# Two mixtures of experts behind an attention: all low weight parts on VectorE, a new order at the begin of a mixture, and one branch less per expert

## The chip, the cores and the metric

The kernel runs on one core of a Trainium2 chip. The metric is the device time of one execution in microseconds (us), of several executions of the same program, smaller being better. The engines are named as the profile names them: PE (matrix products), PEld (its weight loads), DVE (VectorE), ACT (ScalarE), POOL (GpSimd), SP (the queue that issues the plain DMAs). A q behind a name (PEq, POOLq) is the engine's sequencer, which handles branches and semaphores.

## The reference, cut to what matters

An attention with a learned bias gives 1152 tokens of 512 numbers. They go through two mixtures of experts, one after the other, each with 8 experts, of which each token is sent to one:

```python
logits = xn @ en.T / tau              # second mixture: x @ w_gate
expert_idx = np.argmax(logits, axis=1)
...
for e in range(E):
    mask = expert_idx == e
    h = np.maximum(x[mask] @ w1[e], 0.0)             # 512 -> 1024
    out[mask] = gate_w[mask, None] * (h @ w2[e])     # 1024 -> 512
```

The second mixture takes the first one's output as x, has a gate matrix of its own, and drops tokens over a capacity of 288 per expert. All is float32. How many tokens an expert gets is known only at run time.

## The kernel before, in words

**Stages.** The attention fills about the first 250 us. Its last steps already load and split the first expert's weights (`early`, L918) and route 7 of the 9 token tiles. Then `moe` (L1210) routes the rest, runs the first mixture (`run(0, router)`), computes the second mixture's gate from the rows written (`gate2`, L1168) and runs the second mixture (`run(1, router)`). From L1213 on the order on every engine is the order of the program text.

**High and low parts.** Products are made at near float32 accuracy from a fast format: each weight piece (128 x 1024) is split by `hi` (L886, the rounded copy) and `lo` (L900, the raw piece minus the high part), and each product is the sum of three (`TERMS`, L575: high by high, high by low, low by high). An expert has eight pieces: 0 to 3 are w1, 4 to 7 are w2. The argument `eng` names the engine: A is ACT, V is DVE, G is POOL. `lo` frees its raw buffer and so issues, on SP, the DMA of the same piece of the next expert (`load`, L872). The tokens and the hidden values are split in the same way out of PSUM, always by ACT (high) and DVE (low): `halves` (L943) and `part` (L986).

**One tile.** `tile` (L961) computes up to 128 tokens of one expert: product 1 in two halves (`mm1`), the turn of the hidden values, product 2 (`mm2`, L991), scaling on ACT (L1020) and a scatter by an indirect DMA from POOL (L1027). Between its steps it calls `work(0)` to `work(5)`. In `run` (L1070), `work` splits the pieces of the *next* expert, of which piece 7 goes to POOL (high at step 0, low at step 4) and the others to ACT and DVE. At step 4 `turn` (L939) turns the tokens of the next tiles, and POOL gathers tokens ahead by indirect DMAs (`gather`, L928): the first tile of expert e+2 at step 0, the second tile of expert e+1 at step 4.

**Branches.** Each expert's first tile always runs. A second and further tiles stand in nested `tc.If` blocks (`more`, L1150, the If at L1161), which all engines evaluate; `announce` (L1145) gives PE a hint of the coming branch. Before the first tile, L1138 and L1139 put the gather of a *third* tile under an If of its own.

**Begin of a mixture.** `run` turns the router's result into lists and counts (`lists`, L788), gathers the first tokens, loads the counts into registers (L1078), lets PE run some products for nothing (`warm`) and calls `gates` (L799): an exponential on ACT, then on DVE a sum, a reciprocal and two spreads into `Bv` (`spread`, L716). Just before the second spread the first tile's tokens are turned. PE uses `Bv` in `gates2` (L824), called at step 1 of the first expert's tile, between its two halves of product 1. In the first mixture, the low parts of pieces 3, 6 and 7 of expert 0 go to POOL behind that, those of 4 and 5 to DVE.

**Between the mixtures.** In the last expert's tile of the first mixture, `held` (L877) lets only pieces 4 and 5 be loaded, since the raw buffers 0 to 3 take the first mixture's rows. Pieces 6 and 7 of the second mixture's first expert (number 8) are split at the end of `gate2` (L1195 to L1198) and in `run` (L1090), their low parts on POOL. Right behind them `gate2` calls `choose`, `place` and `spots`, a chain of small DVE instructions that gives the second mixture's lists.

Of the kernel before, what the change touches and what calls it, by code (L numbers as in the profile page):

```python
# [10 lines left out]
F16 = mybir.dt.float16  # L11
# [3 lines left out]
ALU = mybir.AluOpType  # L15
# [3 lines left out]
P = 128  # L19
B, H, S, D = 2, 8, 576, 64  # L20
BH = B * H
E8, FF = 8, 1024
# [548 lines left out]
NTT = NTOK // P  # L571
# [124 lines left out]
class Router:  # L696
# [99 lines left out]
        else:  # L796
            V.tensor_scalar(self.cnt, self.ps[:, 72:80], g.cap, None, ALU.min)

    def gates(self, turn, then):  # L799

        nc, V = self.nc, self.nc.vector
        if self.norms is not None:
            V.tensor_scalar(self.norms, self.norms, 1e-6, None, ALU.add)
            V.reciprocal(self.norms, self.norms)
            V.tensor_tensor(self.d, self.d, self.norms.unsqueeze(2).to_broadcast([P, NTT, E8]), ALU.mult)
        nc.scalar.activation(self.d, self.d, AF.Exp)
        then()
        gt = self.T("gt", [NTT])
        V.tensor_reduce(gt, self.d, AX.X, ALU.add)
        V.tensor_scalar(gt, gt, 1e-9, None, ALU.add)  # L810
        V.reciprocal(gt, gt)
        g2 = self.T("g2", [2, NTT], F16)
        V.tensor_copy(g2[:, 0], gt)
        V.tensor_tensor(gt, gt, g2[:, 0], ALU.subtract)
        V.tensor_scalar(g2[:, 1], gt, 4096.0, None, ALU.mult)
        self.Bg = []
        for j in range(2):
            if j == 1:
                turn()
            V.tensor_tensor(self.oht, self.oh, g2[:, j].unsqueeze(2).to_broadcast([P, NTT, E8]), ALU.mult)  # L820
            self.Bg.append(self.T("Bv", [NTT, E8 * NTT], F16, 2))
            self.spread(self.Bg[j], 0, NTT, self.oht, self.th)

# [15 lines left out]
class Experts:  # L839
# [32 lines left out]
    def load(self, ge, j):  # L872

        if ge >= 2 * E8:
            return
        m, e = divmod(ge, E8)
        w = self.a[("m_w1", "n_w1")[m] if j < 4 else ("m_w2", "n_w2")[m]][e]  # L877
        if self.held is not None and j not in (4, 5):
            return
        q = (ge * 8 + j) % NRAW  # L880
        r = self.raw[ge, j] = (self.rp if q < 6 else self.sp).tile([P, 1024], F32, tag=f"raw{q}", name="raw")
        kc = 1 if j < 4 else 2
        w = w.rearrange("(k p) f -> p k f", p=P)[:, (j % 4) * kc:(j % 4 + 1) * kc, :]
        self.nc.sync.dma_start(r.rearrange("p (k f) -> p k f", k=kc), w)
# [54 lines left out]
    def turn(self, key):  # L939
        if key in self.px:  # L940
            self.px[key] = self.halves(self.px[key], key[0])
# [128 lines left out]
    def run(self, m, router):  # L1070

        nc = self.nc
        A, V, G = nc.scalar, nc.vector, nc.gpsimd
        L = self.lists[m] = router
        L.lists()
        self.gather(m, 0, 0, ("b", 0))
        self.gather(m, 0, 1, ("f", 0))
        _, counts = nc.values_load_multi_w_load_instructions(L.cnt[0:1, :], min_val=0, max_val=NTOK,  # L1078
                                                             skip_runtime_bounds_check_because="numbers of tokens")
        self.warm(m * E8, WARM[m][2])  # L1080
        L.gates(lambda: self.turn(("b", 0)), lambda: m or self.hi(0, 7, A))
        if m == 0:
            self.lo(0, 3, G)
            self.lo(0, 4, V)
            self.lo(0, 5, V)
            self.lo(0, 6, G)
            self.lo(0, 7, G)
        self.held = None
        if m == 1:
            self.lo(E8, 7, G)  # L1090
        self.gather(m, 1, 0, ("b", 1))
        for e in range(E8):
            n = m * E8 + e + 1

            def work(at, e=e, n=n):
                if at == 0:
                    if n == E8:
                        self.held, self.yt = True, []
                    self.hi(n, 0, A)
                    self.hi(n, 1, A)  # L1100
                    self.lo(n, 0, V)
                    self.lo(n, 1, V)
                    if n == E8:
                        self.rows(0)
                        self.rows(1)
                    self.gather(m, e + 2, 0, ("b", e + 2))
                    if e < E8 - 1:
                        self.hi(n, 7, G)
                elif at == 1:
                    if e == 0:  # L1110
                        L.gates2()
                    self.hi(n, 2, A)
                elif at == 2:
                    self.lo(n, 2, V)
                    self.hi(n, 3, A)
                    self.lo(n, 3, V)
                    if n == E8:
                        self.rows(2)
                        self.rows(3)
                        self.rows(4)  # L1120
                    if e == 0:
                        L.gates3()
                elif at == 3:
                    self.hi(n, 4, A)
                elif at == 4:
                    self.hi(n, 5, A)
                    self.lo(n, 4, V)
                    self.turn(("f", e))
                    self.turn(("b", e + 1))
                    self.gather(m, e + 1, 1, ("f", e + 1))  # L1130
                    if e < E8 - 1:
                        self.lo(n, 7, G)
                    self.lo(n, 5, V)
                if at == 4 and e < E8 - 1:
                    self.hi(n, 6, A)
                    self.lo(n, 6, V)

            with self.tc.If(counts[e] > 2 * P):  # L1138
                self.gather(m, e, 2, ("x", 2))  # L1139
            self.announce(m, e, 1, counts[e])  # L1140
            self.tile(m, e, 0, ("b", e), work)
            self.px["x", 1] = self.px.pop(("f", e))
            self.more(m, e, 1, counts[e])
# [24 lines left out]
def gate2(tc, g, ex, router):  # L1168

    nc = tc.nc  # L1170
# [4 lines left out]
    n = len(todo)  # L1175
    x, lT = {}, {}
    for t in range(n + 3):
# [14 lines left out]
        elif u >= 0:  # L1192
            v = u - (u > OWN)
            nc.tensor.transpose(pb[:, v * 16:(v + 1) * 16], lT[u], g.ident[0:16, 0:16])  # L1194
    ex.hi(E8, 6, nc.scalar)  # L1195
    ex.hi(E8, 7, nc.scalar)
    ex.lo(E8, 6, nc.gpsimd)
    ex.release(E8 + 1, [6])  # L1198
    nc.vector.tensor_reduce(router.lg, pv.rearrange("p t a e -> p t e a"), AX.X, ALU.add)
    nc.vector.tensor_tensor(router.lg, router.lg, own, ALU.add)  # L1200
    ex.warm(E8, WARM[1][4])
# [71 lines left out]
```

## Time and profile before

| what | value |
|---|---|
| device time, median of 3 runs | 659.82 us (657.37 to 660.79) |
| the profiled execution's own time | 658.62 us |
| its span, first to last instruction | 656.7 us |
| mean granted clock of PE | 0.966 of full speed |
| busy PE, DVE, ACT, POOL | 551.3, 475.0, 400.8, 343.3 us |

Durations below come from the profiled execution. Its time exceeds its span by 1.9 us, which lie outside the first and last instruction. A timeline line gives start, duration, engine, line of the kernel, operation, tiles written and read, shape, and in brackets the idle time before it with what ended it; "x2" merges instructions that follow each other.

### The profile page before, as it was taken

What the parts mean: (1) busy time and instruction counts of PE and PEld (TensorE: products, weight loads), DVE (VectorE), ACT (ScalarE), POOL (GpSimd) and SP (SyncE); (2) the same over time, 40 slices, a digit from 0 to 9 for tenths busy, and PEclk for the clock granted to TensorE, in tenths of its full rate; (3) what the DMA queues carried; (4) which work ended last, traced back from release to release, by engine and by line L of the source; (5) the groups of instructions that cost most, each with busy time, mean ns of one, the idle gap of its engine ahead of it and who ended that gap; (6) DMA issues with size and microseconds to landing.
All of it is one profiled execution on the core that took longest, in us unless ns stands there. A gap on an engine that the chain in (4) does not pass through costs nothing. (4 is left out here: it accounts for less than half of the span.)

```text
span 656.7 us, 13255 instructions
## 1 busy us (share of the span) xinstructions
PE 551.3 (84%) x4970; PEld 463.6 (71%) x4970; DVE 475.0 (72%) x702; ACT 400.8 (61%) x668; POOL 343.3 (52%) x290
## 2 busy tenths in 40 slices
PE   2446688887898999679999999989979999999892
PEld 2445577887887887467788788767757887777672
DVE  5789999999998886868951371289679725929660
ACT  4566877887888855358742443378527626648451
POOL 3997899988987262634552141144145513525430
PEclk9977988999999999889999999999999999999797
DMA  7922545101100772298971270168737734847700
GB/s 228 308 74 51 142 133 165 38 30 37 25 18 18 164 267 80 81 324 302 326 284 44 59 252 30 35 211 316 276 102 241 277 126 147 302 150 233 267 8 8
DMA packets 46871, 101.46 MB, mean 154 GB/s; under 512 B 10740, under 2 KB 12660, under 8 KB 46496
## 3 DMA queue, kind: packets, MB, share of 16 engines
q1 hardware_dynamic: 40640, 92.12, 43.2%
q0 software_dynamic: 5232, 7.49, 3.3%
q8 instruction: 64, 1.05, 0.7%
q14 instruction: 55, 0.45, 0.2%
q10 hardware_dynamic: 880, 0.35, 0.2%
HBM read 94.06 MB, written 13.67 MB: 164 GB/s over the span
## 5 line engine op out<-in xcount | busy, mean ns | idle before, releaser
L906 DVE TENSOR_TENSOR wl<-raw,wh 128x1024 fp32r<-128x1024 f32 x106 | 155.1, 1499 | 22.4 <-ACT wh L893 17.4
L959 PE MATMUL py<-wh,hT 128*128 128x512 f32 x400 | 141.4, 404 | 0.3 <-DVE hT L989 0.2
L893 ACT CAST wh<-raw 128x1024 fp32r<-128x1024 f32 x111 | 114.8, 1050 | 12.5 <-ACTq L1161 4.4
L989 DVE TENSOR_TENSOR hT<-pt,hT 128x512 fp32r<-128x512 f32 x50 | 34.5, 691 | 92.7 <-ACT hT L988 92.6
L272 POOL TENSOR_TENSOR btmp<-abst,xp 128x256 f32<-128x256 f32 x78 | 81.0, 1038 | 16.4 <-ACT abst L271 15.2
L959 PEld LDWEIGHTS py<-wh,hT 128*128 128x128 f32 x400 | 75.0, 188 | 16.0 <-DVE hT L989 1.1
L259 PE MATMUL pm<-wmov,mask 128*128 128x64 f16 x1296 | 58.7, 204 | 28.4 <-DVE wmov L234 12.3
L959 PE MATMUL py<-wl,hT 128*128 128x512 f32 x200 | 78.2, 391 | 0.0
L259 PEld LDWEIGHTS <-mask 128*128 128x128 f16 x1296 | 52.9, 106 | 33.5 <-DVE mask L246 22.9
L321 PE MATMUL s<-K,Q 128*128 128x288 f32 x320 | 64.2, 326 | 13.8 <-DVE mx L329 10.3
L273 POOL TENSOR_TENSOR bias<-abst,btmp 128x256 f32<-128x256 f32 x78 | 72.0, 923 | 5.8
L246 DVE TENSOR_TENSOR mask<-toep,T 128x1024 f16<-128x1024 f16 x72 | 69.6, 984 | 0.8 <-PE pm L259 0.5
L339 ACT ACTIVATE P<-sb,mx 128x576 f32<-128x576 f32 x72 | 55.8, 776 | 23.0 <-DVE mx L329 19.3
L271 ACT ACTIVATE abst<-pm,swi 128x512 f32<-128x512 f32 x78 | 53.0, 685 | 21.9 <-PE pm L259 20.6
L959 PE MATMUL ph<-wh,xh 128*128 128x512 f32 x120 | 52.1, 434 | 15.6 <-PEq L1161 10.2
L353 PE MATMUL pt<-ident,P 128*128 128x128 f32 x324 | 53.5, 287 | 9.5 <-DVE ptl L364 6.0
L329 DVE CUSTOM_DVE_ANT_0 sb<-s,bias 128x576 f32<-128x576 f32 x72 | 53.7, 748 | 8.0 <-PE s L321 4.5
L364 DVE SCALAR_TENSOR_TENSOR ptl<-pt,pth 128x512 f16<-128x512 f32 x81 | 54.8, 680 | 5.2 <-ACT pth L359 5.0
L321 PEld LDWEIGHTS s<-K,Q 128*128 128x128 f32 x320 | 47.7, 198 | 15.1 <-issue 9.2
L906 POOL TENSOR_TENSOR wl<-raw,wh 128x1024 fp32r<-128x1024 f32 x22 | 52.7, 2398 | 6.2 <-ACT wh L893 5.5
L359 ACT ACTIVATE pth<-pt 128x512 f16<-128x512 f32 x81 | 47.6, 592 | 8.4 <-PE pt L353 7.1
L988 ACT CAST hT<-pt 128x512 fp32r<-128x512 f32 x50 | 29.4, 587 | 34.3 <-PE pt L983 30.4
(216 smaller groups left out, 1191.0 us busy)
## 6 DMA issues: line engine op xcount, KB each, us to landing
raw<-m_w_dram SPq DMA_DIRECT2D x64, 512.0 KB
raw<-n_w_dram SPq DMA_DIRECT2D x64, 512.0 KB
kraw<-a_k_dram SPq DMA_DIRECT2D x16, 288.0 KB
qraw<-a_q_dram SPq DMA_DIRECT2D x16, 256.0 KB
out_dram<-zero SPq DMA_DIRECT2D x9, 256.0 KB
y_tok<-zero SPq DMA_DIRECT2D x9, 256.0 KB
vraw<-a_v_dram SPq DMA_DIRECT2D x2, 1024.0 KB
x_tok<-x SPq DMA_DIRECT2D x8, 256.0 KB
```

Of the source, the lines that this page charges most:

```text
L246: nc.vector.tensor_tensor(m, w, T[:, i0:i0 + P].unsqueeze(1).to_broadcast([P, 8, P]), ALU.is_gt)
L259: nc.tensor.matmul(pm[:, :, :, gq * 4:gq * 4 + 4], m[:, gq], wmov[:, part], start=part == 0, stop=part == 1)
L272: nc.gpsimd.tensor_tensor(tmp, ab_[:, 0], xp, ALU.mult)
L273: nc.gpsimd.tensor_tensor(biases[it][:, :, cs], ab_[:, 1], tmp, ALU.add)
L321: nc.tensor.matmul(ps[:, half, :288], Q[:, part, h], K[:, b * H + h, half * 288:half * 288 + 288], start=i == 0, stop=i == last)
L329: nc.vector.tensor_tensor_reduce(sb.rearrange("p (t j) -> p t j", t=2), o.ps.pop(h)[:, :, :288], biases[o.it][:, h].rearrange("p (t j) -> ...
L339: nc.scalar.activation(o.Pt[hp][:, x * S:(x + 1) * S], sb, AF.Exp, bias=mx, scale=-1.0, accum_out=o.sums[:, h:h + 1])
L353: nc.tensor.transpose(pt[:, cc], src, ident)
L364: nc.vector.scalar_tensor_tensor(tl[:, ccs], o.pt.pop(h)[:, ccs], PSC, th[:, ccs], ALU.mult, ALU.subtract)
L893: eng.copy(hi, r)
L906: eng.tensor_tensor(lo, self.raw.pop((ge, j)), hi.bitcast(F32), ALU.subtract)
L959: self.nc.tensor.matmul(ps, x[a_][:, xs], w[b_][:, ws], start=first and i == 0, stop=last and i == 2)
```

## The change

All low parts in the two mixtures go to DVE. At the begin of the first mixture they are put between the parts of `gates`, which is cut into three. Pieces 6 and 7 of expert 8 are split in the last expert's tile of the first mixture, and their loads' successors are no longer held back there. The third tile's gather stands without an If.

```diff
--- before.py
+++ after.py
@@ -796,7 +796,7 @@
         else:
             V.tensor_scalar(self.cnt, self.ps[:, 72:80], g.cap, None, ALU.min)
 
-    def gates(self, turn, then):
+    def gates_exp(self):
 
         nc, V = self.nc, self.nc.vector
         if self.norms is not None:
@@ -804,20 +804,25 @@
             V.reciprocal(self.norms, self.norms)
             V.tensor_tensor(self.d, self.d, self.norms.unsqueeze(2).to_broadcast([P, NTT, E8]), ALU.mult)
         nc.scalar.activation(self.d, self.d, AF.Exp)
-        then()
+
+    def gates_sum(self):
+
+        nc, V = self.nc, self.nc.vector
         gt = self.T("gt", [NTT])
         V.tensor_reduce(gt, self.d, AX.X, ALU.add)
         V.tensor_scalar(gt, gt, 1e-9, None, ALU.add)
         V.reciprocal(gt, gt)
-        g2 = self.T("g2", [2, NTT], F16)
-        V.tensor_copy(g2[:, 0], gt)
-        V.tensor_tensor(gt, gt, g2[:, 0], ALU.subtract)
-        V.tensor_scalar(g2[:, 1], gt, 4096.0, None, ALU.mult)
+        self.g2 = self.T("g2", [2, NTT], F16)
+        V.tensor_copy(self.g2[:, 0], gt)
+        V.tensor_tensor(gt, gt, self.g2[:, 0], ALU.subtract)
+        V.tensor_scalar(self.g2[:, 1], gt, 4096.0, None, ALU.mult)
+
+    def gates_spread(self):
+
+        V = self.nc.vector
         self.Bg = []
         for j in range(2):
-            if j == 1:
-                turn()
-            V.tensor_tensor(self.oht, self.oh, g2[:, j].unsqueeze(2).to_broadcast([P, NTT, E8]), ALU.mult)
+            V.tensor_tensor(self.oht, self.oh, self.g2[:, j].unsqueeze(2).to_broadcast([P, NTT, E8]), ALU.mult)
             self.Bg.append(self.T("Bv", [NTT, E8 * NTT], F16, 2))
             self.spread(self.Bg[j], 0, NTT, self.oht, self.th)
 
@@ -875,7 +880,7 @@
             return
         m, e = divmod(ge, E8)
         w = self.a[("m_w1", "n_w1")[m] if j < 4 else ("m_w2", "n_w2")[m]][e]
-        if self.held is not None and j not in (4, 5):
+        if self.held is not None and j < 4:
             return
         q = (ge * 8 + j) % NRAW
         r = self.raw[ge, j] = (self.rp if q < 6 else self.sp).tile([P, 1024], F32, tag=f"raw{q}", name="raw")
@@ -1078,16 +1083,23 @@
         _, counts = nc.values_load_multi_w_load_instructions(L.cnt[0:1, :], min_val=0, max_val=NTOK,
                                                              skip_runtime_bounds_check_because="numbers of tokens")
         self.warm(m * E8, WARM[m][2])
-        L.gates(lambda: self.turn(("b", 0)), lambda: m or self.hi(0, 7, A))
+        self.held = None
         if m == 0:
-            self.lo(0, 3, G)
+            self.lo(0, 3, V)
+        L.gates_exp()
+        if m == 0:
+            self.hi(0, 7, A)
             self.lo(0, 4, V)
             self.lo(0, 5, V)
-            self.lo(0, 6, G)
-            self.lo(0, 7, G)
-        self.held = None
-        if m == 1:
-            self.lo(E8, 7, G)
+            L.gates_sum()
+            self.turn(("b", 0))
+            self.lo(0, 6, V)
+            self.lo(0, 7, V)
+            L.gates_spread()
+        else:
+            L.gates_sum()
+            L.gates_spread()
+            self.turn(("b", 0))
         self.gather(m, 1, 0, ("b", 1))
         for e in range(E8):
             n = m * E8 + e + 1
@@ -1104,8 +1116,7 @@
                         self.rows(0)
                         self.rows(1)
                     self.gather(m, e + 2, 0, ("b", e + 2))
-                    if e < E8 - 1:
-                        self.hi(n, 7, G)
+                    self.hi(n, 7, G)
                 elif at == 1:
                     if e == 0:
                         L.gates2()
@@ -1128,15 +1139,12 @@
                     self.turn(("f", e))
                     self.turn(("b", e + 1))
                     self.gather(m, e + 1, 1, ("f", e + 1))
-                    if e < E8 - 1:
-                        self.lo(n, 7, G)
                     self.lo(n, 5, V)
-                if at == 4 and e < E8 - 1:
                     self.hi(n, 6, A)
                     self.lo(n, 6, V)
-
-            with self.tc.If(counts[e] > 2 * P):
-                self.gather(m, e, 2, ("x", 2))
+                    self.lo(n, 7, V)
+
+            self.gather(m, e, 2, ("x", 2))
             self.announce(m, e, 1, counts[e])
             self.tile(m, e, 0, ("b", e), work)
             self.px["x", 1] = self.px.pop(("f", e))
@@ -1192,10 +1200,6 @@
         elif u >= 0:
             v = u - (u > OWN)
             nc.tensor.transpose(pb[:, v * 16:(v + 1) * 16], lT[u], g.ident[0:16, 0:16])
-    ex.hi(E8, 6, nc.scalar)
-    ex.hi(E8, 7, nc.scalar)
-    ex.lo(E8, 6, nc.gpsimd)
-    ex.release(E8 + 1, [6])
     nc.vector.tensor_reduce(router.lg, pv.rearrange("p t a e -> p t e a"), AX.X, ALU.add)
     nc.vector.tensor_tensor(router.lg, router.lg, own, ALU.add)
     ex.warm(E8, WARM[1][4])
```

## Rows read from the trace of the kernel before

**Rows 1.** Busy time by engine in two stretches (PE, PEld, DVE, ACT, POOL), clock, DMA.

```profile
273.70:276.70 3.00, 2.94 (x22) 2.24 (x23) 2.97 (x5) 0.83 (x2) 0.27 (x1) 0.50 0.04 10
...
305.80:319.10 13.30, 13.13 (x64) 10.53 (x64) 12.46 (x12) 10.26 (x15) 7.34 (x6) 1.00 0.90 309
```

**Rows 2.** What PE waited for, 250 to 480 us (total us, times, longest).

```profile
PE ph L959 <- PEq L1161: 5.3, 4, 3.3
PE ph L975 <- DVE xl L954: 5.2, 1, 5.2
...
PE pt L948 <- DVE hT L989: 0.8, 1, 0.8
...
PE ph L959 <- DVE xl L954: 0.5, 1, 0.5
```

**Rows 3.** What PE waited for, 480 to 660 us.

```profile
PE ph L959 <- PEq L1161: 5.0, 4, 3.0
...
PE pr L747 <- DVE oh L742: 2.5, 1, 2.5
```

**Rows 4.** Timeline of PE: begin of the first mixture, and where three experts begin.

```profile
273.76 2.08 PE L975 MATMUL ph<-wh,xl 128*128 128x512 f32 x4 [5.25 <-DVE xl L954]
275.63 1.30 PE L829 MATMUL pr<-Bv,A 128*128 128x72 f16 x18
...
290.51 0.66 PE L959 MATMUL ph<-wh,xh 128*128 128x512 f32 x1 [3.32 <-PEq L1161]
...
305.80 0.49 PE L959 MATMUL ph<-wh,xh 128*128 128x512 f32 x1 [0.66 <-PEq L1161]
...
319.75 0.48 PE L959 MATMUL ph<-wh,xh 128*128 128x512 f32 x1 [0.81 <-ACTq L1161]
```

**Rows 5.** Timeline of DVE at the begin of the first mixture.

```profile
261.60 0.17 DVE L803 TENSOR_SCALAR ss<-ss 128x9 f32<-128x9 f32 x1 [0.97 <-DVE cnt L795]
...
264.37 6.75 DVE L810 TENSOR_SCALAR gt<-gt 128x9 f32<-128x9 f32 x1
...
273.88 0.83 DVE L720 TENSOR_TENSOR Bv<-oht,th 128x648 f16<-128x648 f16 x1
```

**Rows 6.** Timeline of POOL: low parts, a gather, a high part.

```profile
264.06 7.01 POOL L906 TENSOR_TENSOR wl<-raw,wh 128x1024 fp32r<-128x1024 f32 x3
...
428.53 1.04 POOL L934 DMA_INDIRECT xgb<-x_tok,si  x1 [4.51 <-PE pt L983]
429.60 1.07 POOL L895 TENSOR_SCALAR wh<-raw 128x1024 fp32r<-128x1024 f32 x1
...
434.08 2.41 POOL L906 TENSOR_TENSOR wl<-raw,wh 128x1024 fp32r<-128x1024 f32 x1
...
479.49 2.36 POOL L906 TENSOR_TENSOR wl<-raw,wh 128x1024 fp32r<-128x1024 f32 x1 [5.51 <-ACT wh L893]
```

**Rows 7.** Timeline of DVE later on.

```profile
428.97 3.91 DVE L906 TENSOR_TENSOR wl<-raw,wh 128x1024 fp32r<-128x1024 f32 x2
...
433.41 4.18 DVE L906 TENSOR_TENSOR wl<-raw,wh 128x1024 fp32r<-128x1024 f32 x1
...
466.98 0.69 DVE L954 TENSOR_TENSOR xlx<-pt,xhx 128x512 fp32r<-128x512 f32 x1 [2.47 <-ACT xhx L953]
...
479.65 2.29 DVE L739 TENSOR_TENSOR d<-lg,mx 128x72 f32<-128x72 f32 x1
```

**Rows 8.** The low parts by line L906 on DVE: ns min/median/max, first to last start.

```profile
L906 DVE TENSOR_TENSOR wl<-raw,wh x106: 1208/1218/4179, 274.6 to 631.5; 128x1024 fp32r<-128x1024 f32 x106
```

**Rows 9.** The page's costliest groups: busy us, mean ns, idle before.

```profile
L893 ACT CAST wh<-raw 128x1024 fp32r<-128x1024 f32 x111 | 114.8, 1050 | 12.5 <-ACTq L1161 4.4
L989 DVE TENSOR_TENSOR hT<-pt,hT 128x512 fp32r<-128x512 f32 x50 | 34.5, 691 | 92.7 <-ACT hT L988 92.6
```

**Rows 10.** Timeline of ACT at the end of the first mixture.

```profile
464.83 0.69 ACT L1020 ACTIVATE xgf<-py,gs 128x512 f32<-128x512 f32 x1 [2.18 <-PE py L959]
```

**Rows 11.** Line L1138 on PE's sequencer, 299 to 308 us.

```profile
L1138 PEldq COMPARE_BRANCH  x1: 224/224/224, 305.3 to 305.3; - x1
```

## The prediction

> **What bounds the kernel now.** I read the stretches first: in an ordinary tile of the first mixture PE is busy 13.13 of 13.30 us, at full clock [rows 1]. So only time in which PE stands still, or runs at the low clock, can be won in the mixtures, and the next view is what PE waited for. Before 480 us that is 5.2 us for one low part of the first tokens, 5.3 us in four waits behind the branch at L1161, and 0.8 and 0.5 us for DVE [rows 2]; after 480 us it is 5.0 us behind that branch and 2.5 us for the router's chain [rows 3]. Next come the timelines around these waits.
>
> The 5.2 us stand at the begin of the first mixture: PE goes on at 273.76 after an idle 5.25 [rows 4]. DVE was held there by an addition on 9 numbers per partition that took 6.75 us, from 264.37 to 271.12 [rows 5], while POOL ran three low parts in a row from 264.06 to 271.07 [rows 6]. Both ended together: DVE could not start until POOL's run was over. The same shows at the router's chain: L739 took 2.29 us and ended at 481.94 [rows 7], beside POOL's low part of 479.49 to 481.85 [rows 6]. And in the tiles: a low part on DVE takes 1.22 us in the median but up to 4.18 [rows 8]; that longest one started at 433.41 [rows 7], when a low part of POOL was about to start at 434.08 [rows 6], and the waits of 0.8 and 0.5 us [rows 2] lie right behind it.
>
> **The change part by part. Begin of the first mixture.** DVE can start at 261.60 [rows 5]. Its new list is: low part 3, 1.22; three small instructions, 0.7 (estimate, four times the 0.17 of the first [rows 5]); low parts 4 and 5, 2.44; the sum and its followers with the tokens' low part and both spreads; then low parts 6 and 7, 2.44, between these. Freed at 271.12, DVE ended that middle work at 273.88 + 0.83 = 274.71 [rows 5], so it takes 3.6, with 0.4 for the reduction and the addition that come ahead of it 4.0. The sum is 1.22 + 0.7 + 2.44 + 4.0 + 2.44 = 10.8 us, and the last spread ends at 272.4 against 274.71.
>
> The tokens' low part comes out of this at about 268.5, which is when PE wants it (273.76 less 5.25). That wait goes. But PE's next stop is L829, which needs both spreads, and these now stand behind all five low parts: PE gets there near 269.6 and waits until about 272.4. L829 then ends near 272.8, where it ended at 276.7 before (the next product follows 1.1 us behind 275.63 [rows 4]). Of 5.25 us, 3.9 are won and the rest becomes a wait for `Bv`. Against that stands POOL, which in this stretch has four gathers and a high part of piece 7 to issue, each about 1.05 us [rows 6], and these too can hold DVE: two low parts took 3.91 us from 428.97 [rows 7], not 2.4, beside a gather and a high part [rows 6]. Three such holds take 3.1 back. So the bounds are 0.8 and 3.9; I take **2.4**, the middle, since POOL's gathers and DVE's low parts fall in the same 8 us but not all on each other. The clock lies inside this: it was at 0.50 (1.2 GHz) in the 3 us behind the wait [rows 1], and may be so behind the new one. SP gets the loads behind pieces 3 to 7 earlier by these same few us, and the gather of expert 1 no longer stands behind three low parts in POOL's queue; nobody waits for either, so this counts as nothing.
>
> **The rule on that lock.** The rows show DVE waiting out three POOL instructions. The Trainium skill (SBUF — State Buffer, on the shared port pair) says that a VectorE instruction with two SBUF inputs or in a two-port mode and a GpSimd instruction exclude each other, each for the whole of one instruction, whoever starts first. Taken to the letter, DVE would get in after the first of the three, 2.4 us, and a sum by the page would then have about 1.4 us for the begin (2.4 for the wait less the holds of about one short instruction). The trace has 6.75, so here a run of POOL instructions counts as one hold, and my sum goes by that.
>
> **The branch at L1138.** Its compare takes 0.224 us on PE's sequencer at 305.3 [rows 11], inside the 0.66 us that PE stands between two experts [rows 4]. With its neighbours I count 0.25 for each of 14 experts (the first of each mixture waits for its tokens anyway): **3.5**. Lower bound nothing, if another part of the way through L1161 ends last; upper 4.2, at 0.30. In exchange POOL runs the gather for every expert, 1.04 each [rows 6], with all rows out of bounds where there is no third tile. POOL queues behind it the gather of expert e+2 and the high part of piece 7; the gather has a whole tile of 14 us until it is turned, so I cost this at nothing. If that cover went, 1 us per expert would show.
>
> **The router's chain of the second mixture.** L739 was held from 479.65 until POOL ended at 481.85 and ran about 0.1 us beyond that, so 2.2 us of its 2.29 are hold; PE waits for this chain [rows 3], and I count **2.1**. The low part and two ACT casts that stood here go into the tile before. There a cast of 1.05 [rows 9] fits into ACT's idle 2.18 [rows 10], and two low parts, 2.4, fit just into DVE's idle 2.47 before the first tokens of `gate2` [rows 7]. Cost nothing, at most 0.5 if they come later. The two loads that go out earlier stand on SP behind the reads of the rows.
>
> **Piece 7 of the other experts** moves to DVE: 1.22 more per tile. In a tile DVE then has eight low parts, 9.8, and four reads of PSUM at 0.69 [rows 9], 2.8: 12.5 us beside a tile of 13.95 (319.75 less 305.80 [rows 4]). What it loses in work it wins in holds, since a hold by POOL's low part costs 2.4. So nothing, and the waits of 0.8 and 0.5 us [rows 2] go: **1.3**.
>
> **The sum.** 2.4 + 3.5 + 2.1 + 1.3 = 9.3. The profiled execution took 658.62 us, so 649.3; the median of the runs stands 1.2 above that execution, and I take 650.0.
>
> **Rivals.** *The waits behind L1161 change their number.* Two of the branches that skip further tiles cost far more than the others: 3.32 us at 290.51 [rows 4] and one of 3.0 us [rows 3], against 0.66. The tile behind the first took 15.29 us (290.51 to 305.80) where the next took 13.95, so one costs 2.7 + 1.3 = 4.0. All PE code behind the removed branch moves by a few instructions per expert, so these two can go, or others come: one less gives 646, two less 642, one more 654. For it: two of about a dozen show it with the same code, so something as small as place or moment decides. Against: nothing in the change aims at it. The Trainium skill (Runtime: NRT & Kernel Launch, instruction fetch mechanics) has a rule for it: a taken branch whose target is outside the window that is loaded stalls for a fetch. By that rule, a branch whose target lies near costs no fetch, and a sum by the page would have nothing for L1138 and 653 or so; the trace has 0.224 for it.
>
> *DVE becomes the bound of the tiles.* This is the one that ends slower. DVE needs 12.5 us of the 13.7 that a tile then takes. POOL now issues two gathers and a high part of piece 7 in a row in each tile, 3.2 us, and a run of POOL's holds DVE as a whole, as at the begin. It decides from 1.2 us of holds per tile on. If all 3.2 fell on DVE, each of the ten single tiles that prepare a next expert would take 2.0 longer: 650 + 20 = 670. Against: before, DVE carried the same holds and one of 2.4 us besides, and PE hardly waited for it [rows 2].
>
> *The branch was not the last in its gap, or the begin's wait only moves.* Then 3.5 or 2.4 us are missing: 653 or so, with both 656.
>
> *The change does nothing that PE sees,* because all of these gaps are set by something else: 660.
>
> **How the numbers follow.** The forecast (647 to 653) has 0.50; fewer waits at L1161 (640 to 646) 0.17; one more of them (653 to 658) 0.13; branch or begin empty (653 to 657) 0.12; DVE the bound (663 and more) 0.05; nothing 0.03. A measurement can tell 0.5%, 3.3 us, from no change, so faster means below 656.5 and slower above 663.1. Faster: 0.50 + 0.17, most of 0.13 and 0.12, 0.86 in all; same 0.09; slower 0.05. The range that leaves out 0.2 goes from 642, two waits less, to 656, both terms empty or one wait more with a weak begin.
>
> **What would show it.** In the new profile: L810 near 0.2 us; PE's 5.25 gone and a wait of 2 to 3 us at L829 for `Bv` in its place; L739 at a few tenths and PE's 2.5 us for it shorter; gaps of about 0.4 us between experts; low parts on DVE with a longest near 2.3 instead of 4.18. The prediction is wrong if PE waits for `hT` or `xl` in most single tiles, if the gaps stay at 0.66, or if the waits behind L1161 of 3 us are other than two.

## The result, and the profile after

The changed kernel takes 644.36 us (median of 4 runs, 643.15 to 646.07) against 658.6 (657.37 to 660.79) before: a ratio of 0.977, 95% interval [0.974, 0.980], so 14.2 us less. The prediction said 650.0, within 642 to 656. One of all executions reported below, in run 12, had a granted clock of 0.83 and took 676.38 us; it is left out. The profiled execution took 643.15 us, against 658.62. Its page begins so, and further down has the queue of the indirect DMAs:

```profile
span 641.4 us, 13184 instructions
...
PE 546.4 (85%) x4970; PEld 461.5 (72%) x4970; DVE 466.1 (73%) x721; ACT 399.8 (62%) x667; POOL 319.4 (50%) x285
...
q0 software_dynamic: 6272, 7.49, 3.6%
```

DVE has 19 low parts more, some 23 us at 1.22 each, and is still busy 8.9 us *less* (475.0 before): so about 32 us of its busy time before was waiting for POOL. The statistics of its low parts (ns, least, median and greatest, where [rows 8] stands for before) say the same:

```profile
L911 DVE TENSOR_TENSOR wl<-raw,wh x125: 1209/1218/2762, 261.7 to 617.2; 128x1024 fp32r<-128x1024 f32 x125
```

What PE waited for from 250 to 480 us, to be held against [rows 2]:

```profile
PE ph L964 <- PEq L1169: 4.6, 7, 1.7
PE pr L834 <- DVE Bv L720: 2.3, 2, 1.7
PE pt L953 <- DMA yt<-y_tok: 2.1, 1, 2.1
...
PE pr L747 <- DVE oh L742: 1.6, 1, 1.6
PE ph L964 <- issue: 0.8, 1, 0.8
```

and from 480 us to the end, against [rows 3]:

```profile
PE ph L964 <- PEq L1169: 3.2, 7, 0.6
```

No wait for `hT` or a token's low part is left. The two waits of 3 us behind the branch of further tiles (now L1169) are gone: 1.7 is the longest of seven before 480 us, 0.6 after it. In place of the first there are two stops, 1.74 and 0.83 us. New are the waits for `Bv`, which was foreseen, and for rows read back (`yt`), which was not. PE's timeline at the same places as [rows 4]:

```profile
268.40 1.08 PE L980 MATMUL ph<-wh,xl 128*128 128x512 f32 x4
271.14 0.45 PE L834 MATMUL pr<-Bv,A 128*128 128x72 f16 x9 [1.66 <-DVE Bv L720]
272.28 0.45 PE L834 MATMUL pr<-Bv,A 128*128 128x72 f16 x9 [0.68 <-DVE Bv L720]
272.56 0.48 PE L964 MATMUL ph<-wh,xh 128*128 128x512 f32 x1
...
284.61 0.49 PE L964 MATMUL ph<-wh,xh 128*128 128x512 f32 x1 [1.74 <-PEq L1169]
...
288.43 0.50 PE L964 MATMUL ph<-wh,xh 128*128 128x512 f32 x1 [0.83 <-issue]
...
299.13 0.50 PE L964 MATMUL ph<-wh,xh 128*128 128x512 f32 x1 [0.38 <-PEq L1169]
...
456.19 1.09 PE L953 MATMUL pt<-ident,yt 128*128 128x128 f32 x4 [2.14 <-DMA yt<-y_tok]
```

and DVE's at the begin and in the router's chain, as [rows 5, 7]:

```profile
263.43 2.35 DVE L911 TENSOR_TENSOR wl<-raw,wh 128x1024 fp32r<-128x1024 f32 x2
...
265.95 0.17 DVE L813 TENSOR_SCALAR gt<-gt 128x9 f32<-128x9 f32 x1
...
271.39 0.83 DVE L720 TENSOR_TENSOR Bv<-oht,th 128x648 f16<-128x648 f16 x1
...
471.75 0.23 DVE L1204 TENSOR_TENSOR lg<-lg,own 128x72 f32<-128x72 f32 x1 [1.17 <-DMA own<-l_tok]
472.28 0.23 DVE L739 TENSOR_TENSOR d<-lg,mx 128x72 f32<-128x72 f32 x1
```

**Where 15.3 us of span went.** I took the start of every tile's first ACT activation as a mark and compared the intervals between marks. Up to expert 2 the changed kernel gains 6.67 us: 4.18 by the first product behind `Bv` (272.56 against 276.74) and 2.49 around the first skipped branch and the gap behind it. Ten later intervals that hold one plain gap between experts are shorter by 3.32 in all, 0.33 each. Two more, the first tiles of the two experts with four tiles, are shorter by 0.74 together; they hold no such gap. The interval with the low parts of 3.91 and 4.18 us [rows 7] loses 2.09 (15.58 to 13.49), and the one with the second wait of 3 us 5.54 (18.98 to 13.44). Against that, `gate2`'s interval, from the last tile of the first mixture to the first of the second, is 1.68 longer (40.21 to 41.89), and the tail from the last mark to the end 1.35: 6.67 + 3.32 + 0.74 + 2.09 + 5.54 - 1.68 - 1.35 = 15.33, the 15.3 but for rounding.

### The profile page after: what moved, and what is told of

The parts are those of the page before. It is cut to its first block, busy times and chain, and to the rows that moved or that the text cites. A ratio compares the mean times of both kernels' runs of the same rounds, so it can differ in the third digit from the quotient of the medians.

```text
span 641.4 us, 13184 instructions
## 1 busy us (share of the span) xinstructions
PE 546.4 (85%) x4970; PEld 461.5 (72%) x4970; DVE 466.1 (73%) x721; ACT 399.8 (62%) x667; POOL 319.4 (50%) x285
## 3 DMA queue, kind: packets, MB, share of 16 engines
q0 software_dynamic: 6272, 7.49, 3.6%
## 5 line engine op out<-in xcount | busy, mean ns | idle before, releaser
L964 PE MATMUL ph<-wh,xh 128*128 128x512 f32 x120 | 50.1, 418 | 8.6 <-PEq L1169 7.7
L1033 POOL DMA_INDIRECT y_tok<-y,si x13 | 18.0, 1382 | 67.6 <-ACT y L1025 41.1
```

The costliest lines, as they stand in the source:

```text
L964: self.nc.tensor.matmul(ps, x[a_][:, xs], w[b_][:, ws], start=first and i == 0, stop=last and i == 2)
```

## The experiments

In the edits, `third` stands for `self.gather(m, e, 2, ("x", 2))`. Ratios are to executions of the kernel before that ran beside them; a version with one time and no ratio was executed once.

**1. The changed kernel with the branch back.**

```diff
-            third
+            with self.tc.If(counts[e] > 2 * P):
+                third
```

> The new kernel with the third tile's gather under its If again, all else as changed. Account of the two traces: each of 13 gaps between experts is 0.34 longer, 4.4 us; POOL's last drain goes back from 6.5 to about 5.5 us, since it grew with the number of indirect DMAs (13 empty gathers more), so 1.1 less at the end; and the rows for the second gate come about 1 us earlier. On the second wait of 3 us behind the branch over further tiles, which the change lost (5.2 us with its low clock), two theories: by place (PE's code is where it was before again) it returns and the time is about 651; by moment (the order on DVE and POOL decides) it stays away and the time is about 646. Rival of the whole: the branch cost PE nothing, and the time stays at 644.

652.6 us (651.22 to 655.08), ratio to before 0.990 [0.987, 0.993]. PE's timeline has the gaps of 0.66 again, and the second long wait. A wait for `hT` is back too, though every low part is still on DVE:

```profile
427.51 0.66 PE L953 MATMUL pt<-ident,xgb 128*128 128x128 f32 x4 [0.84 <-DVE hT L994]
...
609.13 0.79 PE L964 MATMUL ph<-wh,xh 128*128 128x512 f32 x1 [2.72 <-PEq L1170]
...
626.30 0.49 PE L964 MATMUL ph<-wh,xh 128*128 128x512 f32 x1 [0.66 <-PEq L1170]
```

The interval with the second long wait is 18.64 us (13.44 in the changed kernel), so the theory by place holds; the one with the wait for `hT` is 14.80 (13.49). The span from the last scatter's start to the end falls to 10.6 us, from 12.0.

**2. The kernel before without the branch, and nothing else.**

```diff
-            with self.tc.If(counts[e] > 2 * P):
-                third
+            third
```

> The kernel before with the gather's If taken away and nothing else. 13 gaps of 0.34 less, 4.4 us, and the drain 1.1 longer: about 655. By place, the second wait of 3 us behind the branch over further tiles goes too, and the time is about 650. If the branch was not the last in its gap: 658 to 660.

652.65 us (650.27 to 655.69), ratio 0.990 [0.987, 0.993]: between the two theories. In PE's timeline the second long wait is gone at the same expert, though run 1 has it at 609.13 and this run is there at 610.09, while the first stays:

```profile
290.65 0.49 PE L959 MATMUL ph<-wh,xh 128*128 128x512 f32 x1 [3.01 <-PEq L1160]
...
304.70 0.49 PE L959 MATMUL ph<-wh,xh 128*128 128x512 f32 x1 [0.38 <-PEq L1160]
...
610.09 0.49 PE L959 MATMUL ph<-wh,xh 128*128 128x512 f32 x1 [0.38 <-PEq L1160]
```

So the second wait goes with the branch, whatever the moment: it is there in all three profiles with the branch (before, 1 and 4), and in none of the eleven without it. The interval with POOL's low part of [rows 6] falls to 13.48 by this edit alone. What is missing to the lower theory lies in three intervals in which PE waits for `hT` or the next tile's tokens (0.75 to 1.1 longer than before each, with the one behind the first of them 0.8 longer), in `gate2` (41.51) and in a tail of 12.0. By the spans, the branch alone gains 6.2 us and all the rest of the change (before against run 1) 6.1, both together 15.3.

**3. The changed kernel with the old begin** (low parts 3, 6, 7 of expert 0 on POOL).

```diff
-            self.lo(0, 3, V)
...
-            self.lo(0, 6, V)
-            self.lo(0, 7, V)
...
+            L.gates_spread(lambda: self.turn(("b", 0)))
+            self.lo(0, 3, G)
...
+            self.lo(0, 6, G)
+            self.lo(0, 7, G)
```

> The new kernel with the begin of the first mixture as it was (low parts 3, 6 and 7 of expert 0 on POOL behind the gates, the tokens' turn ahead of the second spread). My account: DVE's addition takes 6.7 us again beside POOL's three low parts, PE waits 5.2 for the tokens' low part and none for the spreads, the first product behind the gates' products starts 4.2 later (276.7 instead of 272.6), and the time is about 648. Rival: the begin's gain is given back at the next branch, where the first wait of 3 us shrank only because of it; then up to 6 us, 650.

653.79 us, more than either theory said. The addition L813 takes 7.63 us and PE waits 5.23. The rest is at the first skipped branch, which waits 3.05, with a second stop in the tile behind it:

```profile
297.52 0.72 PE L966 MATMUL ph<-wh,xh 128*128 128x512 f32 x1 [1.93 <-issue]
```

**4. The kernel before, with only one low part on POOL at the begin.**

```diff
-            self.lo(0, 6, G)
-            self.lo(0, 7, G)
+            self.lo(0, 6, V)
+            self.lo(0, 7, V)
```

> The kernel before with low parts 6 and 7 of expert 0 on DVE behind the gates and only low part 3 on POOL. If DVE is held by each instruction of POOL for itself (page on SBUF), it should have got in after the first of three, so that the 6.75 had another cause and stays near 6.7. If a run of POOL counts as one hold, the hold shrinks to that one low part: the addition takes about 2.3 and PE's wait of 5.25 falls to about 0.8.

655.39 us. DVE's addition and POOL's low part, from the two timelines:

```profile
263.72 2.77 DVE L810 TENSOR_SCALAR gt<-gt 128x9 f32<-128x9 f32 x1
```

```profile
264.08 2.36 POOL L906 TENSOR_TENSOR wl<-raw,wh 128x1024 fp32r<-128x1024 f32 x1
```

Both end at 266.4 to 266.5. With one POOL instruction the hold is 2.77 us, with three in a row 6.75 [rows 5, 6]: a run of them holds as a whole. PE's wait for the token's low part falls from 5.25 to 0.61. But a wait of 2.82 for `hT` comes instead, since DVE now runs six low parts ahead of it.

**5. The changed kernel with the loads of pieces 6 and 7 held back in gate2.**

```diff
-        if self.held is not None and j < 4:
+        if self.held is not None and j not in (4, 5):
...
+    ex.release(E8 + 1, [6, 7])
     nc.vector.tensor_reduce(router.lg, pv...
```

> The changed kernel, but the loads of pieces 6 and 7 of the expert after next are held back until the second router's products are through, as in the kernel before (the casts and low parts stay where the change has them). The changed kernel's stage of gate2 is 1.7 us longer than before (41.9 against 40.2 us), with PE waiting 2.1 us for rows read back from y_tok and DVE 1.2 us for own logits. Theory of the earlier loads: they share the DMA engines with the scatter and the read-back; held back, both waits go and the stage falls to about 40, the run to about 642.5. Rival, the longer POOL queue (an extra gather ahead of expert 6's scatter): the waits stay, the stage stays at 41 to 42, the run at 644.

644.46 us; the stage takes 40.46. The wait for rows stays, and it is now followed by full clock in the table of stretches (the last three numbers are the granted clock, the DMA share and GB/s), where the changed kernel's fell. First the wait in PE's timeline, then the stretch:

```profile
458.76 0.63 PE L953 MATMUL pt<-ident,yt 128*128 128x128 f32 x4 [2.17 <-DMA yt<-y_tok]
```

```profile
458.00:461.00 3.00, 1.75 (x13) 1.34 (x13) 1.84 (x2) 1.07 (x3) 0.34 (x1) 1.00 1.02 357
```

The changed kernel, one stretch around its wait for the rows:

```profile
455.00:458.00 3.00, 1.81 (x8) 1.49 (x9) 1.25 (x2) 0.59 (x1) 0.79 (x1) 0.67 0.88 294
```

The own logits are waited for 0.82 instead of 1.17. So the earlier loads are not what delays the rows.

**6. The changed kernel with the spreads ahead of low parts 6 and 7.**

```diff
+            L.gates_spread()
             self.lo(0, 6, V)
             self.lo(0, 7, V)
-            L.gates_spread()
```

> The changed kernel, but at the begin of the first mixture the two spreads of the gates stand ahead of low parts 6 and 7 on DVE. In the changed kernel PE waits 1.7 + 0.7 us for the spreads, since two low parts of 1.2 us each stand ahead. Theory: this wait is the rest of the begin's cost; with the spreads first it falls to nearly nothing and the low parts are still there in time for the last products of the first tile, so 2 to 2.4 us less, about 642. Rival: the low parts 6 and 7 (or hT, which DVE reads behind them) are then late in the first tile, as with the one-low run, where the wait for hT took 2.8 us: same time, 644.

644.16 us (643.44 to 646.76), ratio to before 0.976 [0.973, 0.979]: no gain. PE's timeline, from the slowest of its executions (646.76), shows where it went:

```profile
271.62 0.45 PE L834 MATMUL pr<-Bv,A 128*128 128x72 f16 x9 [0.29 <-DVE Bv L720]
...
276.77 0.74 PE L964 MATMUL py<-wh,hT 128*128 128x512 f32 x2 [0.93 <-DVE hT L994]
...
285.64 0.49 PE L964 MATMUL ph<-wh,xh 128*128 128x512 f32 x1 [2.19 <-PEq L1169]
...
290.56 0.51 PE L964 MATMUL ph<-wh,xh 128*128 128x512 f32 x1 [1.90 <-issue]
```

The wait for `Bv` falls by 2.0, `hT` is 0.9 late as the rival said, and the two stops at the first skipped branch are 0.45 and 1.07 longer than in the changed kernel, whose PE program is the same.

**7. The third tile's gather moved into the second tile's branch.**

```diff
-            third
...
-                if at == 0 and t > 1:
+                if at == 0:
```

> The changed kernel without the branch around the third tile's gather, and without the gather being issued for every expert: it is issued in the second tile's work, inside the branch that tile has anyway. So PE still has no branch there, but POOL no longer issues a gather with all rows out of bounds where there is no second tile. Theory of the gathers' price: the drain at the end goes from 6.5 back to about 5.6 us and the last INC_SWDGE_SEM from 1.74 to 1.5 (1.0 to 1.2 us of the tail's 1.35), and expert 6's scatter, and so the rows of gate2, come about 1 us earlier: 642 in all, 641 at best. Rival: the third tile's gather now comes a tile later and the tiles behind it wait for it (three experts), and PE's code moves, so that one of the stops of 3 us behind L1169 comes back: 645 or more.

644.63 us (642.19 to 647.33), ratio to before 0.978 [0.975, 0.982]; the profiled execution has 642.19. The page's queue row and PE's timeline:

```profile
q0 software_dynamic: 5312, 7.49, 3.4%
```

```profile
455.44 0.66 PE L953 MATMUL pt<-ident,yt 128*128 128x128 f32 x4 [0.82 <-ACTq L1168]
```

The rows come in time, `gate2` takes 40.73 (41.89), and the tail is 10.9 (12.0). Two intervals in which PE turns a third tile's rows are longer by 0.30 and 0.57, one single tile by 0.28, and DVE waits 1.53 for the own logits (1.17). So both theories hold, and little is left. The queue carries 80 packets for each gather, also for one with all rows out of bounds: the changed kernel has 1040 packets and thirteen gathers more than the kernel before, and 1.35 us more of tail. All profiles agree on that tail: 10.6 us at 5232 packets (three of them), 10.9 at 5312 (three), 11.9 to 12.0 from 6112 to 6272 (eight).

**8. A ninth low part per tile on DVE.**

```diff
-        eng.tensor_tensor(lo, self.raw.pop((ge, j)), hi.bitcast(F32), ALU.subtract)
+        for _ in range(2 if j == 7 and ge > 0 else 1):
+            eng.tensor_tensor(lo, self.raw[ge, j], hi.bitcast(F32), ALU.subtract)
+        self.raw.pop((ge, j))
```

> The changed kernel, with the low part of piece 7 computed twice on DVE for every expert but the first (the second result is the same): 1.2 us more DVE work in each tile that prepares a next expert, 13.7 us of work where a tile takes 13.0. Theory that DVE has little room left in a single tile: ten single tiles become longer by 0.7 us or more each, 7 to 12 us in all, 651 to 656, with PE waiting for hT or xl. Rival, that DVE has a margin of over 1.2 us per tile, since it can run ahead into the tiles that prepare nothing: under 3 us, 644 to 647.

649.42 us. Nearly all single tiles take 13.3 to 13.5 us as in the changed kernel; one of them and the first tiles of two experts with further tiles are 1.0 longer, one 0.5, and `gate2` 1.2. PE's waits for `hT` are short, as this one in its timeline:

```profile
321.22 0.73 PE L966 MATMUL py<-wh,hT 128*128 128x512 f32 x2 [0.57 <-DVE hT L996]
```

In the profile, the span is 6.3 longer, and about 1 of it lies in the begin, where the clock fell. So DVE has a low part's room in most single tiles, and not in two of the four first tiles that further tiles follow.

**9. Edits 5 and 7 together.** (The diffs are those two.)

> The changed kernel with both edits on what gate2 waits for: the third tile's gather issued inside the second tile's branch, and the loads of pieces 6 and 7 of the expert after next held until the second router's products are through. Alone, the first took the wait for the rows from 2.1 to 0.8 us and the tail by 1.1 us down but left the wait for the own logits (1.5); the second kept the clock up in the stage and took the own logits' wait to 0.8. Theory that the two add: stage 39.5 to 40, tail 1.1 shorter, less 0.9 for third tiles that now come late: about 642 and faster than the changed kernel by 2. Rival, that what is won at one wait is lost at the next on the same chain (own logits): stage 40.7 as with the first alone, 643.5.

644.78 us (643.79 to 650.15), ratio to before 0.982 [0.978, 0.985]. `gate2` falls to 38.98, 2.9 less: the two edits add there. DVE does not wait for the own logits any more, and PE's wait for the chain is 0.41:

```profile
473.94 0.19 PE L747 MATMUL pr<-oh,trih 128*128 128x72 f16 x1 [0.41 <-DVE oh L742]
```

It is given back where PE waits for a third tile's rows (0.7 and twice 0.5), in one tile where it waits 0.83 for `hT` (1.05), and at the begin (1.35), where this execution's clock was at 0.69 from 272 to 275 us, and the changed kernel's at full.

**10. The same, with the spreads between low parts 6 and 7.**

```diff
             self.lo(0, 6, V)
-            self.lo(0, 7, V)
             L.gates_spread()
+            self.lo(0, 7, V)
```

> The same as the run with both gate2 edits, and at the begin the spreads of the gates stand between low parts 6 and 7 (both ahead of the spreads in the changed kernel, both behind them in the run that had no gain). Theory that the spreads' wait falls from 2.3 to about 1.2 and hT is not late: 1.0 to 1.2 less than the run with both gate2 edits, 641. Rival, that PE, which then comes 1.1 us sooner to the first skipped branch, waits there and at the stop in the next tile for the same moment: no gain, 642.

644.05 us (643.09 to 647.03), ratio 0.979 [0.976, 0.983]. The wait for `Bv` is 1.12 in two parts, the first skipped branch takes 1.66 with no second stop (so the rival is not seen), and `gate2` takes 38.83. The intervals that wait for a third tile's rows give 1.9 back, two tiles 1.35, one of them waiting for `hT`, and the attention ahead of it all took 1.5 longer in this execution.

**11. Only expert 6 of the first mixture without the extra gather.**

```diff
-            third
+            if (m, e) != (0, 6):
+                third
...
-                if at == 0 and t > 1:
+                if at == 0 and (t > 1 or (m, e) == (0, 6)):
```

> The changed kernel, but for expert 6 of the first mixture alone the third tile's gather is issued inside its second tile's branch (it has no second tile, so the gather isn't issued). It tells whether the wait for the rows in gate2 comes from that one gather, which stands on POOL's queue shortly ahead of the scatter whose rows are read back, or from the sum of them. Theory of the one gather: the wait for the rows falls from 2.1 us to 0.8 as before, the tail is shorter by only 0.08, and no third tile is late, so about 643. Rival: the wait stays at 2, 644.4.

649.26 us; the wait for rows stays, 1.98. So that gather is not what makes the rows late. POOL's timeline shows that nothing on POOL delayed the scatter's start: POOL stood idle for 1.46 us and waited for ACT. It starts 11.04 us behind its tile's mark, as in run 7 (11.06) and sooner than in the changed kernel (11.73), but takes 1.97 us.

```profile
442.61 2.02 POOL L900 TENSOR_SCALAR wh<-raw 128x1024 fp32r<-128x1024 f32 x1 [6.87 <-DVE hT L994]
444.79 1.08 POOL L939 DMA_INDIRECT xgf<-x_tok,si  x1 [0.16 <-issue]
447.33 1.97 POOL L1033 DMA_INDIRECT y_tok<-y,si  x1 [1.46 <-ACTq L1170]
```

Most of the extra time is at the first skipped branch, with stops of 2.10 and 2.71.

**12. Edit 5, the spreads as in run 10, and the gather moved for the last two experts of the first mixture only.**

```diff
-            third
+            if m or e < 6:
+                third
...
-                if at == 0 and t > 1:
+                if at == 0 and (t > 1 or not (m or e < 6)):
```

> The changed kernel with the loads held in gate2, the spreads between low parts 6 and 7 at the begin, and the third tile's gather moved into the second tile's branch for experts 6 and 7 of the first mixture only, so that the third tiles elsewhere are gathered as early as in the changed kernel. In the run with the move for all experts gate2 fell from 41.9 to 38.8 us and the begin (two intervals) from 32.8 to 31.7, and late third tiles gave 3.3 back. Theory that the three are separate: gate2 39 to 40.5, begin 31.7 or up to 1.5 more where the clock falls, intervals of the third tiles as in the changed kernel, tail 0.1 less; 641 to 642 and so 2 to 3 below the changed kernel. Rival, that the gathers that stay put the gather and high part ahead of expert 6's scatter in the wrong order again (as with expert 6 alone moved, where the wait for the rows stayed at 2.0): gate2 40.5, begin's gain lost to the stops behind the first skipped branch, 644.

644.35 us (640.96 to 645.25), ratio to before 0.977 [0.974, 0.979]. Third tiles are in time, PE does not wait for the rows, and `gate2` takes 40.5, but the two intervals around the first skipped branch take 3.35 us more than in the changed kernel:

```profile
285.20 0.49 PE L964 MATMUL ph<-wh,xh 128*128 128x512 f32 x1 [2.34 <-PEq L1170]
...
290.42 0.79 PE L964 MATMUL ph<-wh,xh 128*128 128x512 f32 x1 [2.21 <-issue]
```

None of these versions beats the changed kernel by more than the measurement can tell.

## Why the prediction was right, and where it was not

**The sign and the mechanism hold.** The holds of POOL on DVE were read rightly, though not every wait behind them (below, on the tiles). L810's 6.75 us became 0.17, L739's 2.29 became 0.23, and PE's 5.25 us went, with a wait for `Bv` of 2.3 in its place (forecast: 2 to 3). The longest low part on DVE is 2.76 us, where 2.3 was forecast for 4.18. Runs 3 and 4 show by size that the hold follows POOL's run: 7.63 and 6.75 us beside three instructions, 2.77 beside one. By the rule of the Trainium skill (SBUF — State Buffer, SBUF: two separate sides) each instruction excludes the other engine for itself, and DVE would get in between two of them; beside a run, these traces do not show that.

**Begin: 4.2 instead of 2.4, over the upper bound of 3.9.** The list of instructions on DVE was right to 0.2 us: the last spread ended at 272.2, forecast 272.4. The step that failed is "three such holds take 3.1 back". DVE's five low parts took 1.23, 2.35 (two) and 2.35 (two), with POOL's five gathers beside them from 261.44 to 268.13, each 0.3 us apart, so a gather alone does not hold DVE here. In [rows 6, 7] the two low parts of 3.91 us stood beside a gather *and* a high part straight behind it. The changed kernel has the same pair once more, and the hold reaches from DVE's start inside the gather to the end of the high part (DVE, then POOL):

```profile
261.68 1.23 DVE L911 TENSOR_TENSOR wl<-raw,wh 128x1024 fp32r<-128x1024 f32 x1 [1.07 <-issue]
...
484.25 3.90 DVE L911 TENSOR_TENSOR wl<-raw,wh 128x1024 fp32r<-128x1024 f32 x2 [0.26 <-ACT wh L898]
```

```profile
261.44 1.26 POOL L939 DMA_INDIRECT xgb<-x_tok,si  x1 [2.71 <-DVE cnt L795]
...
483.83 1.00 POOL L939 DMA_INDIRECT xgb<-y_tok,si  x1 [0.30 <-issue]
484.86 1.06 POOL L900 TENSOR_SCALAR wh<-raw 128x1024 fp32r<-128x1024 f32 x1
```

That it is the high part that makes the difference is argued from these rows, and was not tried alone.

**Branch: 0.33 per gap instead of 0.25.** The gap fell from 0.66 to 0.38, and the ten plain intervals by 3.32 us: 4.6 for the fourteen gaps, where 3.5 were forecast. The 0.224 us of the compare were the right row; the neighbours cost more than the estimate. The Trainium skill (Runtime: NRT & Kernel Launch, Instruction fetch mechanics) has a stall for a taken branch whose target lies outside the pages that are loaded. No run here shows such a fetch at the removed branch, and it still was not free. Run 2 shows 0.24 to 0.45 in these intervals with nothing else changed.

**Waits in the tiles: 1.75 instead of 1.3,** by the interval around the 4.18 us hold (15.58 to 13.49) less one gap, and 0.74 in the two first tiles. But the reading behind the 1.3 was in part wrong. The wait of 0.8 us ended before POOL's low part began at 434.08; before the change PE's row is this:

```profile
433.54 0.66 PE L948 MATMUL pt<-ident,xgb 128*128 128x128 f32 x4 [0.84 <-DVE hT L989]
```

It lies behind the 3.91 us beside the gather and the high part, which the change leaves on POOL. Runs 1 and 2 tell the two apart: with the branch back and all low parts on DVE the 0.84 stays and only the 0.5 goes (interval 14.80); without the branch and with the low part on POOL both are gone (13.48). Without the branch POOL has one gather more in its queue there, so that its high part starts 5.2 us behind the tile's mark instead of 3.6, when DVE's two low parts are nearly over (422.72 against 422.92). So taking the branch away was enough for this gain; moving the low parts alone gave 0.8 of it (15.58 to 14.80).

**Router's chain: -2.1 forecast, +1.7 measured.** This is the step that was wrong in kind. L739 did lose its hold, but the sentence that cost the moved work and the extra gathers at nothing looked at engines and not at the landing of DMAs. Two things came late instead: the rows written by expert 6's scatter, for which PE waited 2.14, and the own logits, for which DVE waited 1.17. The rows are read back 9.2 us behind the scatter's start (442.79 to 452.03), where it was 7.4 before and 6.9 in run 7. The earlier loads are not the cause (run 5), and the extra gathers at most in part: they put the scatter off by 0.7 us, but run 2 has them all and reads back after 7.0 us with no wait for rows, while runs 1, 10 and 11 have none at expert 6 and wait 1.61, 1.48 and 1.98. What goes with the wait in all fourteen profiles is the scatter's own time on POOL: 1.93 to 2.02 us in the seven with it, 1.02 to 1.82 in the seven without. In the changed kernel DVE had begun a low part just ahead of the scatter, in run 7 just behind it (first two rows and last two):

```profile
442.62 1.21 DVE L911 TENSOR_TENSOR wl<-raw,wh 128x1024 fp32r<-128x1024 f32 x1
442.79 1.93 POOL L1033 DMA_INDIRECT y_tok<-y,si  x1 [0.30 <-issue]
...
442.77 1.22 DVE L911 TENSOR_TENSOR wl<-raw,wh 128x1024 fp32r<-128x1024 f32 x1
442.67 1.07 POOL L1033 DMA_INDIRECT y_tok<-y,si  x1 [2.33 <-ACTq L1168]
```

So a low part that DVE has begun can hold POOL's scatter, by about 0.9 us here: the moved work did cost something, in the direction that the prediction did not look. Why the rows then also land later behind the scatter's end stays open. The earlier loads cost the own logits 0.35 (run 5), and 1.5 where the rows come in time (the wait of 1.53 in run 7 is gone in run 9). Runs 9 and 10 show that 1.2 to 1.4 of the 2.1 us were there to be had: with both edits the stage takes 38.8 to 39.0.

**The tail, 1.35 us, was not in the sum at all.** "I cost this at nothing" covered POOL's issue of the gathers, and POOL has the time. But the end of the program is later the more indirect DMAs there were: the last 10.6 us became 12.0, with thirteen gathers more. Of that, 1.3 us lie in two last steps on POOL's sequencer: INC_SWDGE_SEM took 1.74 us instead of 1.49, and the DRAIN behind it 6.52 instead of 5.46.

**The rival of fewer waits came true, at 0.17 against 0.50 for the forecast.** The second wait of 3 us went, worth 5.2 us beyond the gap rather than 4.0: the clock behind it was at 0.50 for 6.8 us, from 614.95 to 621.78, and behind the first for 3.4. The first became shorter, worth about 1.8. By its own list the prediction was wrong on this point: the waits of 3 us were to stay two, and there is none. The runs settle one of the two: 1 and 2 show that the second wait comes and goes with the branch that was removed. Whether it is the branch itself or where it puts the code behind it, and why that stalls, is not shown by these traces. The first one does not follow PE's program alone: its two stops add up to 2.6 us in the changed kernel and 4.1 in run 6, which changes only DVE's order, and over the runs without the branch to between 1.7 (run 10) and 5.0 (run 3). What sets them is open.

**DVE as the bound did not come,** and run 8 gives the margin: one more low part per tile leaves most single tiles as they are.

By its own terms the sum was 9.3 and should have been 4.2 + 4.6 + 1.75 + 0.75 - 1.7 = 9.6, and with the two rival terms, 5.2 + 1.8, and the tail, 1.35, 15.3, the measured span. The sum hit by errors that cancelled: 4.1 too little at begin, branch and waits, 3.8 too much at the router's chain. (The 650.0 was 0.5 below that sum's own 649.3 + 1.2.) That the time lies in the stated range is due to the rival: 644.36 is outside the 647 to 653 of the forecast, and the 5.6 us below 650 are the waits that the rival had, less the tail.

## What to carry to other kernels

When an instruction on nearly no data takes microseconds, lay the other engines' timelines beside it, look which one ends at the same moment, and move the work that held it. When work is "free" because an engine has room, follow also what it puts on a queue: who waits for the DMA behind it, and what the program waits for at its end. And when a wait is won near the begin, look at the next stop on the same engine before counting it: here gains of 1 to 2 us were lost again at one stop right behind them.

## What was not expected of the hardware

A gather whose rows are all out of bounds costs the queue the same 80 packets as a full one, and the end of the program 0.1 us in the mean: 1.35 us for thirteen (10.6 to 12.0 from the last scatter's start). The fourteen profiles agree on the time by the number of packets, whatever else was changed. A scatter on POOL took up to 2.0 us instead of 1.0 when a low part had begun on DVE just ahead of it. And the clock at one place differs between executions with the same PE code: behind the wait for `Bv`, from 272 to 275 us, it was 1.00 in the changed kernel and in runs 6 and 7, and 0.50 to 0.72 in runs 5, 8, 9 and 11, where that interval is 1 to 2 us longer. What decides it is not shown.
